# Last-factor products moved from VectorE to GpSimd, and a first load that no fill precedes, in a gated linear attention + multiplicative FFN kernel

## The chip, the cores and the metric

The kernel runs on one core of one Trainium2 chip. The time is device microseconds of one execution, as the median over several runs; beside it there is one profiled execution, whose trace gives every instruction's start and duration. Engines: PE is TensorE (PEld its weight loads), DVE is VectorE, ACT is ScalarE, POOL is GpSimd, SP is SyncE, which issues all of this kernel's DMAs.

## The reference

Two blocks in float32. The first is a gated linear recurrence over 768 positions for 4 x 8 heads of size 48; its result, laid out as 3072 rows of 384, goes through a feed-forward block that multiplies two up-projections.

```python
f = 1.0 / (1.0 + np.exp(-f_logit))
for t in range(S):
    state = f[:, :, t, :, None] * state + np.einsum('bhd,bhe->bhde', k[:, :, t], v[:, :, t])
    y[:, :, t] = np.einsum('bhd,bhde->bhe', q[:, :, t], state)
x = y.transpose(0, 2, 1, 3).reshape(B * S, H * D)
a = x @ w1
b = x @ w2
return ((a * b) @ w3) @ w_out
```

w1, w2, w3 and w_out come as float64 and are turned to float32 on the chip.

## The kernel before

The recurrence is cut into 24 chunks `u` of 128 positions, six to a batch (`NCH`). In a chunk, two heads share a tile: one on partitions 0 to 47, the other on 64 to 111, four such pairs side by side in 512 columns. Rows 48 to 63 between them belong to no head and are filled once: the loads' tiles `fs` with 30 (a gate of 1), `ks` and `qs` with 0.

**A chunk's steps**, each a task with a short name:

- `lf`, `lk`, `lq`, `lv`: loads of f_logit, k, q, v on SP's queue (`load`, L357 to L361, one DMA for each half of the partitions, issued at L360).
- `g`: the sigmoid on ACT into `gate` (L385). Two gate tiles alternate.
- `p`, `i`, `r`: a forward scan of products on VectorE (L393), a reciprocal of its last column (L403), a backward scan (L415). `l` copies the last column of the forward scan, the chunk's last factors, into `lasts` on ACT (L398).
- `q`, `k`: q and k scaled by the scans, on VectorE (L409; L424 in the first four chunks, L430 and L431 later).
- `a`, `t`: products of k and q, and transposes of k, on TensorE (L444, L456, L468). `m` copies the products to SBUF on ACT (L540, L543), `c` masks them causally on GpSimd (L549), `e` copies the transposed k (L568).
- `v`, `s`: values and the state's share on TensorE (L490, L502, L509), and the state's update into PSUM (L523).
- `d`: the new state `S` on VectorE, for all but the last chunk of a batch (`state`, L635 to L644). It first forms `G`, 112x4 numbers, the chunk's last factors times the first column of the next chunk's gates (L638). In the first chunk of a batch it multiplies the update by G (L641). In the others it adds the old S to the update (L643) and multiplies the sum by G (L644). `b` copies S into block form `sb` on ACT (L653), which the next chunk's state share reads.
- `y`, `z`, `x`: the result leaves PSUM (L663), is rearranged (L692 on TensorE for the first four chunks, through DRAM by DMAs later), and lands in `xt` (L697 or L687).

**The FFN** works on blocks of four chunks. Weights arrive as 64-bit words (L1093) and are decoded piece by piece: two steps on ACT (L1112, L1115) and four on VectorE (L1118, L1119, L1123, L1129). w3 and w_out are folded into one matrix `wc` (L1176, L1183). L714 issues nearly all FFN products; the first block uses plain products, later blocks a seven-product scheme whose sums are on VectorE (L784, L841, L852, L856, L950, L1208, L1222).

**The order** of all instructions is written by a planner (`Plan`, L75 to L150). Every task has an engine, an estimated cost, tasks that it depends on and a priority, its due time. `order` repeatedly takes the task that could start earliest, and of those that tie the one with the lowest priority number. The tasks are then emitted in that order, and each engine runs its own in order. In the task list, `d` costs 0.55 or 0.9 on VectorE, `c` 1.2 or 1.9 on GpSimd; `past(u, n, ...)` names tasks of the chunk n before, for buffers that are used again. Where TensorE has a planned gap in the first 35 planned us (`FULL`), the emission puts filler products there (L1278 to L1282, instruction at L277), one for each 0.43 planned us; nine stand at the very start. A matrix product in float32 is two instructions in the trace.

**Set-up** (`setup`, L284 to L310) is emitted ahead of all tasks: fills on GpSimd (L287 to L295), the identity matrix, constants on VectorE (L296 to L302), and on GpSimd a permutation matrix, filled (L304) and written in ten copies (L310).

**Who queues behind whom.** SP issues the loads in the planned order, the first f load ahead of everything. GpSimd's queue has only the set-up and then the masks `c`. `g` of chunk u waits for `d` of chunk u - 3, which read the same gate tile.

Of the kernel before, what the change touches and what calls it, by code (L numbers as in the profile page):

```python
# [50 lines left out]
R = 64 + D  # L51
# [138 lines left out]
def rows(par):  # L190
    return slice(64 * par, 64 * par + D)
# [15 lines left out]
def ranged(ctx, tc, q, k, f_logit, v, w1, w2, w3, w_out, out, ident, w12, wc, left):  # L207
# [76 lines left out]
    def setup():  # L284
        nc.scalar.activation(warm, nc.const_aps.tensor(0.0, (R, 1), F32), AF.Sigmoid)
        for i in range(2):
            nc.gpsimd.memset(fs[i][32:64], 30.0)  # L287
            nc.gpsimd.memset(ks[i][32:64], 0.0)
            nc.gpsimd.memset(qs[i][32:64], 0.0)
            if i == 0:  # L290
                make_identity(nc, ident)
        nc.gpsimd.memset(early[32:64, 2:4], 30.0)
        nc.gpsimd.memset(early[32:64, 0:2], 0.0)
        nc.gpsimd.memset(qs[2][32:64], 0.0)
        nc.gpsimd.memset(qs[3][32:64], 0.0)  # L295
        nc.vector.memset(floor, FLOOR)  # L296
        nc.vector.memset(heads(floor)[:, :, 0], 1.0)
        nc.vector.memset(back, 0.0)
        for t in gate:
            nc.vector.memset(t[:, NQ : NQ + 1], 0.0)  # L300
        for t in sb:
            nc.vector.memset(t, 0.0)  # L302

        nc.gpsimd.memset(perm, 0.0)  # L304
        for i, (kc, hp) in enumerate(met):
            for par in range(2):
                for r, t, at_, n in runs(2 * hp + par):
                    if t == kc:
                        a = 64 * par + at_
                        nc.gpsimd.tensor_copy(perm[:, i, r : r + n], ident[0:R, a : a + n])  # L310
# [19 lines left out]
    def past(u, n, *names):  # L330
        return [tk[u - n][nm] for nm in names if u >= n and nm in tk[u - n]]
# [20 lines left out]
    def front(u):  # L352
# [3 lines left out]

        def load(dst, src):  # L357
            def emit():
                for par in range(2):
                    nc.sync.dma_start(dst[rows(par)], src[u, par])  # L360
            return emit  # L361
# [22 lines left out]
        def gates():  # L384
            nc.scalar.activation(gate[u % 2][:, 0:NQ], fu, AF.Sigmoid)  # L385

        t["g"] = plan.add("ACT", 0.65, gates, [t["lf"]] + past(u, 2, "r") + past(u, 3, "d"), n0)
        if u % NCH and "d" in tk[u - 1]:
            tk[u - 1]["d"]["deps"].append(t["g"])

        def forward():
            s["P"] = one.tile([R, NQ], F32, name="fwd")
# [195 lines left out]
    def rest(u):  # L588
# [43 lines left out]
                paired(u + 1)  # L632

        if not closes:
            def state():  # L635
                s["S"] = work.tile([R, HP, D], F32, name="S")
                s["G"] = work.tile([R, HP], F32, name="G")
                nc.vector.tensor_tensor(s["G"], lasts[:, u], heads(gate[(u + 1) % 2][:, 0:NQ])[:, :, 0], ALU.mult)  # L638
                gain = s["G"].unsqueeze(2).to_broadcast([R, HP, D])
                if opens:  # L640
                    nc.vector.tensor_tensor(s["S"], s["pd"], gain, ALU.mult)  # L641
                else:
                    nc.vector.tensor_tensor(s["S"], s["pd"], st[u - 1]["S"], ALU.add)  # L643
                    nc.vector.tensor_tensor(s["S"], s["S"], gain, ALU.mult)  # L644

            t["d"] = plan.add(
                "DVE", 0.55 if opens else 0.9, state, [t["s"], t["l"]] + [tk[u + 1][nm] for nm in "g" if nm in tk[u + 1]] + past(u, 2, "b"), n0,
                frees=[] if u < NPE else [t["s"]],
            )

            def blocks():
                for par in range(2):
                    nc.scalar.copy(sb[u % 2][rows(par), :, 64 * par : 64 * par + D], s["S"][rows(par)])  # L653

            t["b"] = plan.add("ACT", 0.75, blocks, [t["d"]] + past(u, 1, "v"), n0)
# [967 lines left out]
```

## Time and profile before

| what | value |
|---|---|
| median of 4 runs | 489.72 us (489.52 to 489.87) |
| profiled execution | 489.65 us, span 487.8 us |
| VectorE: L638, the product G | x20, 131/155/1071 ns (min/median/max) |
| VectorE: L644 and L643, state | x16 at 357/358/359 ns; L643 mean 353 (x13) and 346 (x3) |
| VectorE: scans L393, L415 | x24 each, mean 1243 and 1234 ns |
| GpSimd: set-up copies L310 | x10, 191/218/1139 ns |
| GpSimd: masks L549 | 64x256 x80, mean 583 ns; 128x1024 x4, mean 1114 ns |

The span is what the profiler recorded of the program, from the first instruction to the last; the execution's time is 1.8 us longer. Of an engine's row in the groups, the duration is what the profiler recorded for one instruction, waits inside it for anything shared included; idle time in front of an instruction is shown with what released it.

### The profile page before, as it was taken

Reading aid. Unit: us, or ns where it says so; the run is one execution under the profiler, and the core shown is the slowest. Engines: PE = TensorE matmul, PEld = TensorE weight load, DVE = VectorE, ACT = ScalarE, POOL = GpSimd, SP = SyncE. Lnnn points to the kernel's source line nnn. Section 1 sums busy time; section 2 is a strip of 40 time slices with the busy share of each in tenths; the row PEclk is TensorE's granted clock in tenths of the full one; section 3 lists DMA queues with packets and bytes.
Section 4 is the critical chain, followed back from the end, with each engine's and each line's share of the span. In section 5 each row is a group of like instructions: output and inputs, shape, how many; then the busy total and the mean of one; then the engine's idle time right before and its main releaser. Section 6 shows DMA issues by size and latency. Waiting matters only on the chain.

```text
span 487.8 us, 9560 instructions
## 1 busy us (share of the span) xinstructions
PE 478.0 (98%) x3696; PEld 408.9 (84%) x3696; DVE 360.1 (74%) x721; ACT 166.0 (34%) x380; POOL 61.7 (13%) x115
## 2 busy tenths in 40 slices
PE   8899999999999999999999999999999999999995
PEld 7788744666799888899988888998899888889995
DVE  7999999999997689689877867456663667664541
ACT  4688456573234442544433441001100110110000
POOL 9110000305202111221311201000000000000000
PEclk9999999999999999999999999999999999999998
DMA  6889467563326553346542103000021000000011
GB/s 179 276 317 270 129 245 256 212 184 82 81 79 168 164 134 110 82 130 170 160 124 56 34 19 97 32 34 0 8 60 50 16 1 0 1 1 0 34 66 40
DMA packets 44920, 50.00 MB, mean 102 GB/s; under 512 B 15426, under 2 KB 34370, under 8 KB 43842
## 3 DMA queue, kind: packets, MB, share of 16 engines
q1 hardware_dynamic: 44866, 49.30, 33.8%
q8 instruction: 31, 0.51, 0.4%
q14 instruction: 23, 0.19, 0.1%
HBM read 40.63 MB, written 8.65 MB: 101 GB/s over the span
## 4 chain that ended last, share of the span: by engine, by line
PE 86%; DVE 6%; issue 1%; DVEq 0%
PE f L714 69%; PE f L1176 4%; PE py L490 4%; PE pa L456 2%; PE py L509 2%; PE py L468 2%; DVE place L1208 1%; PE f L523 1%; DVE place L1123 1%; DVE place L1129 1%; DVE bwd L415 1%; PE f L692 1%; DVE fwd L393 1%; DVE place L1222 0%; DVE place L950 0%
## 5 line engine op out<-in xcount | busy, mean ns | idle before, releaser
L714 PE MATMUL f<-xt,w 128*128 128x256 f32 (+1 forms) x600 | 159.0, 396 | 0.0
L714 PEld LDWEIGHTS f<-xt,w 128*128 128x128 f32 x600 | 113.5, 190 | 24.7 <-issue 10.8
L714 PE MATMUL f<-place 128*128 128x192 f32 (+1 forms) x504 | 112.4, 350 | 0.3 <-DVE place L950 0.3
L714 PEld LDWEIGHTS f<-place 128*128 128x128 f32 x504 | 87.9, 190 | 6.4 <-DVE place L950 0.6
L549 POOL TENSOR_SCALAR_AFFINE_SELECT A<-A 64x256 f32<-64x256 f32 (+1 forms) x84 | 49.4, 608 | 231.8 <-PE py L468 105.6
L1176 PE MATMUL f<-place 128*128 128x384 f32 x128 | 42.6, 489 | 0.5 <-DVE place L1129 0.5
L817 ACT COPY a<-f 128x256 f32<-128x256 f32 x36 | 13.4, 372 | 81.5 <-PE f L714 69.6
L1176 PEld LDWEIGHTS f<-place 128*128 128x128 f32 x128 | 23.9, 190 | 17.3 <-DVE place L1129 1.1
L714 PE MATMUL f<-xt,place 128*128 128x256 f32 x144 | 37.1, 380 | 0.0
L714 PE MATMUL f<-wc,ab 128*128 128x192 f32 x192 | 35.1, 326 | 0.0
L714 PEld LDWEIGHTS f<-wc,ab 128*128 128x128 f32 x192 | 32.0, 190 | 0.4
L393 DVE TENSOR_TENSOR_SCAN fwd<-gate,floor 112x512 f32<-112x512 f32 x24 | 29.8, 1243 | 2.4 <-ACT gate L385 1.9
L543 ACT COPY A<-pa 64x256 f32<-64x256 f32 (+1 forms) x60 | 24.3, 439 | 20.2 <-PE pa L456 19.6
L415 DVE TENSOR_TENSOR_SCAN bwd<-gate,back 112x512 f32<-112x512 f32 x24 | 29.6, 1234 | 0.7
L714 PEld LDWEIGHTS f<-xt,place 128*128 128x128 f32 x144 | 26.6, 189 | 3.5 <-DVE place L784 0.2
L841 DVE TENSOR_TENSOR place<-f,a 128x256 f32<-128x256 f32 x36 | 15.1, 421 | 18.8 <-PE f L714 18.5
L653 ACT COPY sb<-S 48x192 f32<-48x192 f32 x40 | 14.0, 350 | 27.5 <-DVE S L644 18.2
L490 PEld LDWEIGHTS py<-A,vt 128*64 128x64 f32 (+1 forms) x320 | 17.5, 129 | 6.7 <-issue 6.2
L1112 ACT ACTIVATE place<-place 128x512 f32<-128x512 f32 (+2 forms) x24 | 21.3, 888 | 3.9 <-DVE w L1129 2.0
L490 PE MATMUL py<-A,vt 128*64 128x128 f32 (+1 forms) x320 | 22.6, 281 | 0.0
L1115 ACT ACTIVATE place<-place 128x512 f32<-128x512 uint32 (+2 forms) x24 | 21.4, 896 | 1.4 <-DMA place<-in_w_out_dram 1.4
L714 PE MATMUL f<-place,w 128*128 128x256 f32 x72 | 21.4, 379 | 0.0
(119 smaller groups left out, 634.6 us busy)
## 6 DMA issues: line engine op xcount, KB each, us to landing
place<-in_w_dram SPq DMA_DIRECT2D x8, 1024.0 KB, 4.8
place<-in_w_dram SPq DMA_DIRECT2D x12, 512.0 KB, 9.5
out_dram<-o SPq DMA_DIRECT2D x24, 192.0 KB, 1.9
q<-in_q_dram SPq DMA_DIRECT2D x46, 96.0 KB, 2.3
f<-in_f_logit_dram SPq DMA_DIRECT2D x44, 96.0 KB, 2.3
k<-in_k_dram SPq DMA_DIRECT2D x44, 96.0 KB, 2.3
yt<-ys SPq DMA_DIRECT2D x40, 96.0 KB, 2.1
xt<-yt SPq DMA_DIRECT2D x20, 192.0 KB, 2.6
```

Of the source, the lines that this page charges most:

```text
L393: nc.vector.tensor_tensor_scan(s["P"], gate[u % 2][:, 0:NQ], floor, 0.0, ALU.mult, ALU.max)
L415: nc.vector.tensor_tensor_scan(s["R"][:, ::-1], gate[u % 2][:, NQ:0:-1], back[:, ::-1], 0.0, ALU.mult, ALU.max)
L490: nc.tensor.matmul(y_block(u, b)[64 * half : 64 * half + w], lhsT=s["v"][:, h * D : h * D + w], rhs=s["A"][:, par, hp], start=zone not in ...
L543: nc.scalar.copy(parts_of(s["A"].rearrange("p r h c -> p (r h c)"))[p0:p1, :, f], parts_of(s["pa"].rearrange("p r n -> p (r n)"))[p0:p1, : ...
L549: nc.gpsimd.affine_select(out=a, in_=a, pattern=pattern, compare_op=ALU.is_ge, fill=0.0, base=0, channel_multiplier=-1,)
L653: nc.scalar.copy(sb[u % 2][rows(par), :, 64 * par : 64 * par + D], s["S"][rows(par)])
L714: nc.tensor.matmul(out_, lhsT=lhs[i], rhs=rhs[i], start=start and i == 0, stop=i == len(lhs) - 1, skip_group_check=True,)
L817: nc.scalar.copy(q["a"], q["X"])
L841: nc.vector.tensor_tensor(ups["u3", k], q["Y"], q["a"], ALU.add)
L1112: nc.scalar.activation(m, hi.bitcast(F32), AF.Abs)
L1115: nc.scalar.activation(lo.bitcast(F32), lo, AF.Copy, bias=2.0, scale=2.0**-51)
L1176: nc.tensor.matmul(w3s["p", jc], lhsT=w3s[jc][:, kc * P : kc * P + P], rhs=wos[:, kc], start=(kc == 0), stop=(kc == KF - 1),)
```

## The change

The product G is taken out of `state` and becomes a GpSimd task of its own, `G`, with planned cost 0.3. It depends on `l`, on the next chunk's `g` if that is already in the list, and on `d` of two chunks before (its buffer). `d` depends on `s` and `G`; its planned cost falls to 0.36 or 0.72. Where `g` waited for `d` of three chunks before, or was added later to the previous `d`, it is now `G`.

In set-up, the fill of fs[0] is dropped: the first chunk's f load writes rows 0 to 63 in one DMA, the last 16 of them copies of the second half's first rows, and rows 64 to 111 in another. The fill of fs[1] now follows the identity. The fills of ks[1] and qs[1] move from GpSimd to VectorE.

```diff
         for i in range(2):
-            nc.gpsimd.memset(fs[i][32:64], 30.0)
-            nc.gpsimd.memset(ks[i][32:64], 0.0)
-            nc.gpsimd.memset(qs[i][32:64], 0.0)
             if i == 0:
+                nc.gpsimd.memset(ks[i][32:64], 0.0)
+                nc.gpsimd.memset(qs[i][32:64], 0.0)
                 make_identity(nc, ident)
+            else:
+                nc.gpsimd.memset(fs[i][32:64], 30.0)
...
         for t in gate:
             nc.vector.memset(t[:, NQ : NQ + 1], 0.0)
+        nc.vector.memset(ks[1][32:64], 0.0)
+        nc.vector.memset(qs[1][32:64], 0.0)
         for t in sb:
             nc.vector.memset(t, 0.0)
...
         def load(dst, src):
             def emit():
+                if dst is fs[0] and u == 0:
+
+                    nc.sync.dma_start(dst[0:64], src[u].rearrange("two d n -> (two d) n")[0:64])
+                    nc.sync.dma_start(dst[rows(1)], src[u, 1])
+                    return
                 for par in range(2):
                     nc.sync.dma_start(dst[rows(par)], src[u, par])
             return emit
...
-        t["g"] = plan.add("ACT", 0.65, gates, [t["lf"]] + past(u, 2, "r") + past(u, 3, "d"), n0)
-        if u % NCH and "d" in tk[u - 1]:
-            tk[u - 1]["d"]["deps"].append(t["g"])
+        t["g"] = plan.add("ACT", 0.65, gates, [t["lf"]] + past(u, 2, "r") + past(u, 3, "G"), n0)
+        if u % NCH and "G" in tk[u - 1]:
+            tk[u - 1]["G"]["deps"].append(t["g"])
...
         if not closes:
+            def gains():
+                s["G"] = work.tile([R, HP], F32, name="G")
+                nc.gpsimd.tensor_tensor(s["G"], lasts[:, u], heads(gate[(u + 1) % 2][:, 0:NQ])[:, :, 0], ALU.mult)
+
+            t["G"] = plan.add(
+                "POOL", 0.3, gains, [t["l"]] + [tk[u + 1][nm] for nm in "g" if nm in tk[u + 1]] + past(u, 2, "d"), n0,
+            )
+
             def state():
                 s["S"] = work.tile([R, HP, D], F32, name="S")
-                s["G"] = work.tile([R, HP], F32, name="G")
-                nc.vector.tensor_tensor(s["G"], lasts[:, u], heads(gate[(u + 1) % 2][:, 0:NQ])[:, :, 0], ALU.mult)
                 gain = s["G"].unsqueeze(2).to_broadcast([R, HP, D])
...
             t["d"] = plan.add(
-                "DVE", 0.55 if opens else 0.9, state, [t["s"], t["l"]] + [tk[u + 1][nm] for nm in "g" if nm in tk[u + 1]] + past(u, 2, "b"), n0,
+                "DVE", 0.36 if opens else 0.72, state, [t["s"], t["G"]] + past(u, 2, "b"), n0,
                 frees=[] if u < NPE else [t["s"]],
             )
```

## The prediction

> **What bounds the kernel now.** I read first the page's busy shares and its groups, then the tensor engine's waits, then a table of stages, then the first 36 us in order of time.
>
> ```profile
> PE 478.0 (98%) x3696; PEld 408.9 (84%) x3696; DVE 360.1 (74%) x721; ACT 166.0 (34%) x380; POOL 61.7 (13%) x115
> ```
>
> TensorE is busy all the time, so an edit on VectorE or GpSimd pays only where TensorE stops or does nothing useful. The table of stages says where (columns: stretch, its length, then busy time and count for PE, PEld, DVE, ACT, POOL, then clock and DMA):
>
> ```profile
> 8.30:35.50 27.20, 25.34 (x296) 21.86 (x295) 25.46 (x41) 19.75 (x41) 8.20 (x14) 1.00 0.88 292
> 35.50:77.00 41.50, 41.50 (x147) 27.51 (x147) 38.39 (x69) 25.75 (x43) 0.00 (x0) 1.00 0.70 218
> 77.00:135.00 58.00, 57.14 (x407) 36.92 (x405) 55.86 (x73) 29.29 (x54) 15.21 (x20) 1.00 0.50 155
> 135.00:482.40 347.40, 347.39 (x2834) 317.26 (x2834) 234.72 (x529) 88.28 (x239) 30.93 (x64) 1.00 0.23 64
> ```
>
> From 135.0 to 482.4 TensorE never stops (347.39 of 347.40). From 35.5 to 135 it stops 0.86 us in all. In 8.3 to 35.5 it stops 1.86 us, and its busy time there includes the filler multiplications of L277, 2.43 us at 10.68 and 1.04 us at 28.53: 1.86 + 2.43 + 1.04 = 5.3 us is all that this opening holds. The granted clock is 1.00 in all four rows. So the question is when the first up-projection (L714) can start, now 35.45.
>
> The opening in order of time, VectorE, GpSimd, ScalarE and SP together (start, duration, engine, line, operation):
>
> ```profile
> 0.81 0.52 POOL L287 MEMSET f<- 32x512 f32 x1 [0.29 <-POOLq L1610]
> 1.35 0.87 SPq L360 DMA_DIRECT2D f<-in_f_logit_dram  x2
> 4.08 0.63 ACT L385 ACTIVATE gate<-f 112x512 f32<-112x512 f32 x1 [1.77 <-DMA f<-in_f_logit_dram]
> 4.75 1.22 DVE L393 TENSOR_TENSOR_SCAN fwd<-gate,floor 112x512 f32<-112x512 f32 x1 [1.63 <-ACT gate L385]
> ...
> 7.97 4.07 POOL L310 COPY ab<-ident 112x48 f32<-112x48 f32 x10
> ...
> 12.13 1.09 POOL L549 TENSOR_SCALAR_AFFINE_SELECT A<-A 128x1024 f32<-128x1024 f32 x1
> 12.18 1.59 DVE L424 TENSOR_TENSOR K<-k,bwd 112x512 f32<-112x512 f32 x1
> ...
> 17.72 1.18 POOL L549 TENSOR_SCALAR_AFFINE_SELECT A<-A 128x1024 f32<-128x1024 f32 x1 [4.50 <-ACT A L540]
> 17.87 1.05 DVE L638 TENSOR_TENSOR G<-lasts,gate 112x4 f32<-112x4 f32 x1
> 18.84 0.34 DVE L643 TENSOR_TENSOR S<-py,S 112x192 f32<-112x192 f32 x1
> ...
> 24.19 1.09 POOL L549 TENSOR_SCALAR_AFFINE_SELECT A<-A 128x1024 f32<-128x1024 f32 x1 [5.29 <-ACT A L540]
> 24.23 1.07 DVE L638 TENSOR_TENSOR G<-lasts,gate 112x4 f32<-112x4 f32 x1
> ```
>
> The reader is to see two things. The first load is issued at 1.35, as the fill ends (0.81 + 0.52 = 1.33), and every gate, scan and scaling hangs on it. And a VectorE operation with two SBUF inputs that begins beside a GpSimd mask (L549) ends only after it: G takes 1.05 and 1.07 us where it takes 0.13 alone (11.64), K 1.59 where it takes 0.69. L643, which reads PSUM and SBUF, ran 0.34 at the tail of a mask. TensorE's view has what that costs:
>
> ```profile
> 19.24 0.60 PE L468 MATMUL py<-ident,K 112*128 112x112 f32 x4 [0.52 <-DVE S L643]
> ...
> 30.10 1.09 PE L490 MATMUL f<-A,place 128*64 128x128 f32 x16 [0.53 <-POOL A L549]
> ```
>
> **The change, part by part.** Times are of the profiled execution (489.65 us, span 487.84; the runs' median 489.72 is 0.07 above it).
>
> *First load.* Without the fill, SP is free at about 0.81, when ACT and POOL run their first instruction: the load moves 0.54 earlier at most, 0 if SP starts later; I take 0.5. SP issues its loads one behind another (0.42 us each, no pause up to 4.5), so k, q, v and the weights move too; their fills stay ahead of them (ks[0] now ends at 1.33, needed at 1.8). The first of the two DMAs grows from 48 to 64 rows, 32 KB on 192 KB, at the 2.3 us of an f load under 0.1 us. VectorE gets two fills in its place, like L298 0.49 each: its setup ends at 3.11 + 0.97 = 4.08, and the first scan now wants it at 4.75 - 0.5 = 4.25. The wait for the gate hides them with 0.17 to spare; without that cover they cost up to 0.97. TensorE hides 0.1 to 0.4 of the gain at first: its fillers of L277 run to 8.3, and the first transposes start at 8.34 either way.
>
> *G on GpSimd, its own price.* The trace has no two-input operation on GpSimd. From below: the copy L310 unblocked, 0.19; from above the same copy behind a scan, 1.14 (its maximum). I take 0.22, as 112x4 is smaller than those copies. G needs only lasts and the next gates, both there one to seven us before S, so in steady state its cost is 0 on the path; hidden by the update's matmuls, which S needs anyway.
>
> *G(0)* is the exception: it queues behind the ten setup copies, which now end at 12.05. Three fills less (3 x 0.46 = 1.4) bring them to 10.7, but copies wait for scans, so I take 11.4. Then G(0) ends at 11.6, and S(0), which VectorE could take at 11.72 - 0.5 = 11.2, starts at 11.65 instead of 11.90. K(1) comes at 12.0, finds mask(0) running (11.7 to 12.8) and ends near 13.3, not 13.77: turn(1) on TensorE gains **0.5**. Worst case: copies still end at 12.05, gain 0. Best: K(1) starts before the mask and ends at 12.2, gain 0.8, TensorE's own wait there.
>
> *G(1).* Its 1.05 us block goes: S(1)'s first half reads PSUM and runs at once. Turn(2) waits for that half (0.52), now for TensorE's z(0) instead: another **0.5**, sum 1.0. The second half (L644, two SBUF inputs) is late next: it waits out the mask in G's place, which delays only sb(1) on ACT, by then 1 us ahead.
>
> *G(2).* S(2) ended at 25.96, sb(2) went at 26.05 on ACT, and xt (0.48), a decode (0.69) and A(3) stood in order behind it, A(3) at 27.89. With VectorE 1 us earlier and no G, S(2) waits for mask(2) only and ends near 24.6; A(3) is then held by pairs(3) (26.2 - 1.0) and ACT's 0.48 + 0.73 behind it: start near 26.0, mask(3) ends at 28.2 instead of 30.05. TensorE's turn(3) and two fillers take until 28.1 to 28.5. So values(3) gains 1.6 at most; I take **0.5** on top of 1.0, because the decode may still stand ahead of A(3) (0.69).
>
> *Is the gain caught later?* The up-projection's second weights are the next late thing: the sixth decoded piece ends at 39.82 (L1129) and four products of 1.29 us after 35.45 need it at 40.6: 0.8 spare. Decoding is back to back on VectorE from 29.5 (2.12 a piece); it moves by VectorE's own gain, at least 1 us. 1.5 passes.
>
> *From 36 on.* VectorE loses 20 G's, 4.8 us, nearly all where TensorE never waits: 0. GpSimd gains 20 operations, 4.4 us, on an engine 13% busy; each can hold a two-input VectorE operation 0.22. In 77 to 135 that is three or four G's, under 0.9 us, on an engine that loses 0.16 for each: I take 0. The two stops (0.53 at 82.2, 0.34 at 134.7) stay: 0 to -0.87.
>
> *The planner.* VectorE's entry for S falls by 0.18 or 0.19, so a hand-made order is computed anew. The gap before turn(1), five fillers of 0.49, may lose one; I take 0.
>
> Sum: -(0.5 + 0.5 + 0.5) = -1.5. Span 486.3, run 488.15, against the median 488.2. Faster than 0.2% (0.98 us, about what a measurement of this kernel can tell from no change) begins at 488.74.
>
> The Trainium skill, SBUF — State Buffer, section "SBUF: two separate sides", says that VectorE with two SBUF inputs and a GpSimd operation that reads SBUF take one port pair in turns, the later one waiting out the whole instruction. The rows above agree (1.05 for 0.13), and the rule speaks against this change also: a G on GpSimd is one more such holder. GPSIMD Engine Reference, "4.1 Engine selection", puts two-input elementwise work on VectorE, GpSimd being about 2x slower; by it G would take an estimated 0.3 (2 x 0.155), and the sum would stay -1.5, since only G(0) is near the path.
>
> **Rivals.**
> *Nothing arrives* (0.25). G(0) stays behind the copies until 12.27, S(0) runs at 12.3 against 11.90, K(1) still meets the mask, and each later block moves from G to L644; the load's 0.5 is all that is left, or less. For it: ten copies in 4.07 us though one takes 0.22. Against: TensorE waited for L643, not L644. 489.0 to 489.8.
> *The new order costs in the decode stage* (0.15). Between 107.4 and 135 VectorE works 95% of the time and TensorE already waits 0.34 for L950: no slack. If the planner sets one chunk's two scans (1.24 + 1.24) ahead of the sums L1222 and L950, TensorE waits 2.5 longer: -1.5 + 2.5 = +1.0, 490.7. It decides once more than 1.5 us moves ahead. Against: scans stand in that order already.
> *More than the sum* (0.11). A filler goes (0.49) and both later stops close (0.87): 489.72 - 1.5 - 1.4 = 486.9.
>
> **How the numbers follow.** Forecast 0.49, own range 487.6 to 489.0 (a third of the sum either way). Of it 0.45 is faster by over 0.2%; with 0.11 from the larger gain and 0.03 from the top of "nothing" 0.59 faster; 0.26 same; 0.15 slower. The range for 8 in 10 reaches from the larger gain to the reorder: 486.9 to 490.7.
>
> **What would show it.** First f load near 0.85 and first scan near 4.25; turn(1) near 13.4; L638 on POOL at about 0.2 each; no VectorE operation over 1 us beside a mask in front of L643; values(3) near 28.6 and L714 from 34.0; busy shares past 36 as they are. Wrong, if G(0) ends after 12, if L714 starts after 35, or if TensorE's waits for VectorE between 77 and 135 grow past 1 us.

## The result, and the profile after

| | before | after |
|---|---|---|
| median of the runs | 489.72 us (60 runs) | 488.93 us (40 runs) |
| profiled execution | 489.65 us, span 487.8 | 488.89 us, span 486.6 |
| TensorE's last instruction ends | 482.40 | 481.02 |
| first up-projection product on TensorE | 35.55 | 34.80 |
| time of the execution less TensorE's end | 7.25 | 7.87 |

The ratio is 0.9985, with a 95% interval of 0.9981 to 0.9989: faster by 0.79 us, about half of the 1.5 us that were forecast, and inside the 0.2% that the prediction called no change. The table says in short where the rest is. TensorE ends 1.38 us sooner, nearly the forecast; 0.75 of it comes from the opening. Then 0.62 us go again *behind* TensorE's end, where the prediction had not looked. 1.38 - 0.62 = 0.76, the difference of the two profiled executions.

In the new file G is L645, the state's two halves are L657 and L658, the masks L557, the scaling of k L432, of q L417, the products of k and q L452, the values L498, the up-projection L728. First the busy shares:

```profile
PE 476.1 (98%) x3690; PEld 407.2 (84%) x3690; DVE 360.7 (74%) x703; ACT 166.0 (34%) x380; POOL 85.8 (18%) x132
```

VectorE lost 20 G's for two fills and its busy time did not fall (360.1 before); GpSimd's rose by 24 us for operations forecast at 4.4. The table of stages, cut at nearly the same places of the work (columns as before: length, then busy time and count for PE, PEld, DVE, ACT, POOL, then clock and DMA):

```profile
8.30:34.75 26.45, 23.53 (x288) 20.75 (x289) 25.16 (x39) 19.96 (x42) 9.53 (x15) 1.00 0.90 299
34.75:76.25 41.50, 41.50 (x147) 27.53 (x147) 38.56 (x68) 25.31 (x43) 1.48 (x2) 1.00 0.73 219
76.25:134.00 57.75, 57.57 (x410) 37.43 (x409) 55.94 (x73) 29.94 (x55) 17.15 (x22) 1.00 0.52 158
134.00:481.02 347.02, 347.02 (x2833) 316.50 (x2831) 234.46 (x514) 87.83 (x237) 50.24 (x77) 1.00 0.23 64
```

The opening is 0.75 shorter, although TensorE idles longer in it (26.45 - 23.53 = 2.92, before 1.86): the planner's new order has six filler instructions fewer, three fillers of 0.49. The decode stage idles 57.75 - 57.57 = 0.18 where it idled 0.86. The long last stage is as long as before: its row is 0.38 shorter because the cut at 134.00 lies 0.38 later in the work (TensorE's end is 1.38 sooner, and 135.00 - 1.38 = 133.62). Now the opening in order of time, lines of GpSimd, SP, ScalarE, VectorE and TensorE. As in the prediction, turn(n), pairs(n), values(n) and z(n) are TensorE's steps `t`, `a`, `v` and `z` of chunk n, mask(n) is GpSimd's `c`, and K(n), Q(n), S(n) and A(n) are tiles of chunk n.

```profile
0.82 0.59 SPq L364 DMA_DIRECT2D f<-in_f_logit_dram  x1
1.46 0.56 SPq L365 DMA_DIRECT2D f<-in_f_logit_dram  x1
...
4.18 0.63 ACT L393 ACTIVATE gate<-f 112x512 f32<-112x512 f32 x1 [1.87 <-DMA f<-in_f_logit_dram]
4.84 1.22 DVE L401 TENSOR_TENSOR_SCAN fwd<-gate,floor 112x512 f32<-112x512 f32 x1 [0.45 <-ACT gate L393]
...
6.58 5.25 POOL L313 COPY ab<-ident 112x48 f32<-112x48 f32 x10
...
11.80 0.19 POOL L645 TENSOR_TENSOR G<-lasts,gate 112x4 f32<-112x4 f32 x1
11.94 1.08 POOL L557 TENSOR_SCALAR_AFFINE_SELECT A<-A 128x1024 f32<-128x1024 f32 x1
12.03 0.36 DVE L655 TENSOR_TENSOR S<-py,G 112x192 f32<-112x192 f32 x1 [0.22 <-POOL G L645]
12.30 1.27 DVE L432 TENSOR_TENSOR K<-k,bwd 112x512 f32<-112x512 f32 x1
...
13.72 0.57 PE L476 MATMUL py<-ident,K 112*128 112x112 f32 x4 [1.05 <-DVE K L432]
```

The load is issued 0.53 sooner and lands no sooner. The set-up copies start earlier (6.58 instead of 7.97), but the ten take 5.25 instead of 4.07: five of them stand beside a scan or a scaling and take 0.66 to 1.18 each, where three did (0.69, 1.14, 1.14); G(0) starts at 11.80, and turn(1) at 13.72 against 13.91. Then chunks 1 and 2:

```profile
17.53 1.12 POOL L557 TENSOR_SCALAR_AFFINE_SELECT A<-A 128x1024 f32<-128x1024 f32 x1 [0.56 <-ACT A L548]
17.62 0.35 DVE L657 TENSOR_TENSOR S<-py,S 112x192 f32<-112x192 f32 x1
18.07 0.79 DVE L658 TENSOR_TENSOR S<-S,G 112x192 f32<-112x192 f32 x1
18.37 0.55 PE L476 MATMUL py<-ident,K 112*128 112x112 f32 x4
18.79 0.68 DVE L417 TENSOR_TENSOR Q<-q,fwd 112x512 f32<-112x512 f32 x1
...
19.61 1.16 PE L452 MATMUL pa<-Q,K 48*128 48x128 f32 x16 [0.70 <-ACT sb L667]
...
22.00 1.15 POOL L557 TENSOR_SCALAR_AFFINE_SELECT A<-A 128x1024 f32<-128x1024 f32 x1 [3.35 <-ACT A L548]
22.30 1.40 DVE L432 TENSOR_TENSOR K<-ab,bwd 112x512 f32<-112x512 f32 x1
...
24.45 1.16 PE L452 MATMUL pa<-Q,K 48*128 48x128 f32 x16 [1.00 <-DVE Q L417]
...
25.47 0.36 DVE L658 TENSOR_TENSOR S<-S,G 112x192 f32<-112x192 f32 x1
...
26.66 1.01 ACT L548 COPY A<-pa 128x1024 f32<-128x1024 f32 x1
```

S(1)'s first half no longer stands behind a blocked G, and turn(2) comes at 18.37 against 19.24: 0.87 ahead. That lead is not kept in full. The mask of chunk 1 now holds S(1)'s second half (0.79 for 0.36), and behind it Q(2) and the copy sb(1) start 0.43 later; the new order has put pairs(2), which reads Q(2), next on TensorE, and TensorE waits 0.70 there. The mask of chunk 2, which blocked G(2) before, now blocks K(3), which had been free:

```profile
23.02 0.69 DVE L424 TENSOR_TENSOR K<-ab,bwd 112x512 f32<-112x512 f32 x1
```

That is the line of before; K(3) takes 1.40 now, TensorE waits a whole microsecond for Q(3) behind it, and values(3) starts at 29.35 against 30.10, 0.75 ahead. The up-projection has the same 0.75.

### The profile page after: what moved, and what is told of

It is laid out like the page before. It is cut to its first block, busy times and chain, and to the rows that moved or that the text cites. A ratio compares the mean times of both kernels' runs of the same rounds, so it can differ in the third digit from the quotient of the medians.

```text
span 486.6 us, 9566 instructions
## 1 busy us (share of the span) xinstructions
PE 476.1 (98%) x3690; PEld 407.2 (84%) x3690; DVE 360.7 (74%) x703; ACT 166.0 (34%) x380; POOL 85.8 (18%) x132
## 4 chain that ended last, share of the span: by engine, by line
PE 88%; DVE 7%; POOL 2%; issue 1%; DVEq 0%; POOLq 0%
PE f L728 70%; PE f L1190 5%; PE py L498 4%; PE pa L464 2%; PE py L517 2%; PE py L476 2%; DVE place L1222 1%; PE f L531 1%; POOL ab L313 1%; DVE bwd L423 1%; DVE fwd L401 1%; PE f L706 1%; DVE Q L417 1%; DVE place L1137 0%; DVE place L1236 0%
## 5 line engine op out<-in xcount | busy, mean ns | idle before, releaser
L728 PE MATMUL f<-xt,w 128*128 128x256 f32 (+1 forms) x600 | 159.0, 396 | 0.0
L728 PEld LDWEIGHTS f<-xt,w 128*128 128x128 f32 x600 | 113.5, 190 | 24.8 <-issue 10.3
L728 PE MATMUL f<-place 128*128 128x192 f32 (+1 forms) x504 | 112.6, 350 | 0.2 <-DVE place L964 0.2
L728 PEld LDWEIGHTS f<-place 128*128 128x128 f32 x504 | 87.6, 190 | 6.2 <-DVE place L964 0.5
L557 POOL TENSOR_SCALAR_AFFINE_SELECT A<-A 64x256 f32<-64x256 f32 (+1 forms) x84 | 59.5, 728 | 90.4 <-ACT A L551 49.9
L831 ACT COPY a<-f 128x256 f32<-128x256 f32 x36 | 13.4, 372 | 85.0 <-PE f L728 66.0
L728 PE MATMUL f<-xt,place 128*128 128x256 f32 x144 | 37.3, 382 | 0.0
L728 PE MATMUL f<-wc,ab 128*128 128x192 f32 x192 | 35.1, 326 | 0.0
L645 POOL TENSOR_TENSOR G<-lasts,gate 112x4 f32<-112x4 f32 x20 | 14.3, 715 | 102.7 <-ACT lasts L406 39.8
L728 PEld LDWEIGHTS f<-wc,ab 128*128 128x128 f32 x192 | 32.0, 190 | 0.4
L728 PEld LDWEIGHTS f<-xt,place 128*128 128x128 f32 x144 | 26.6, 189 | 4.0 <-DVE place L855 0.5
L498 PEld LDWEIGHTS py<-A,vt 128*64 128x64 f32 (+1 forms) x320 | 17.5, 129 | 6.6 <-issue 6.1
L498 PE MATMUL py<-A,vt 128*64 128x128 f32 (+1 forms) x320 | 22.6, 280 | 0.0
L1129 ACT ACTIVATE place<-place 128x512 f32<-128x512 uint32 (+2 forms) x24 | 21.2, 889 | 1.8 <-DMA place<-in_w_out_dram 1.8
```

The lines of the kernel that those rows point to most:

```text
L498: nc.tensor.matmul(y_block(u, b)[64 * half : 64 * half + w], lhsT=s["v"][:, h * D : h * D + w], rhs=s["A"][:, par, hp], start=zone not in ...
L557: nc.gpsimd.affine_select(out=a, in_=a, pattern=pattern, compare_op=ALU.is_ge, fill=0.0, base=0, channel_multiplier=-1,)
L645: nc.gpsimd.tensor_tensor(s["G"], lasts[:, u], heads(gate[(u + 1) % 2][:, 0:NQ])[:, :, 0], ALU.mult)
L728: nc.tensor.matmul(out_, lhsT=lhs[i], rhs=rhs[i], start=start and i == 0, stop=i == len(lhs) - 1, skip_group_check=True,)
L1129: nc.scalar.activation(lo.bitcast(F32), lo, AF.Copy, bias=2.0, scale=2.0**-51)
```

## The experiments

Time less TensorE's end means, below, the profiled execution's time minus the end of its last matmul. Up-projection means its first instruction on TensorE. Both come from one execution of each kernel, and the opening differs from one execution to the next: before, before_pad and one_swap have the same instructions up to there, and reach the up-projection at 35.55, 35.77 and 35.37. So a difference of 0.3 there is not clear of chance by itself. The ratios come from all the runs.

### Taking the change apart

**setup_only**: the set-up and the first load alone, with G on VectorE inside `state` and the old order.

```diff
-            nc.gpsimd.memset(fs[i][32:64], 30.0)
-            nc.gpsimd.memset(ks[i][32:64], 0.0)
-            nc.gpsimd.memset(qs[i][32:64], 0.0)
             if i == 0:
+                nc.gpsimd.memset(ks[i][32:64], 0.0)
+                nc.gpsimd.memset(qs[i][32:64], 0.0)
                 make_identity(nc, ident)
+            else:
+                nc.gpsimd.memset(fs[i][32:64], 30.0)
...
+                if dst is fs[0] and u == 0:
+                    nc.sync.dma_start(dst[0:64], src[u].rearrange("two d n -> (two d) n")[0:64])
+                    nc.sync.dma_start(dst[rows(1)], src[u, 1])
+                    return
```

> The set-up part alone, G still on VectorE, the old order of tasks kept instruction for instruction. If the prediction's step on the first load holds (0.54 us earlier, handed on): first sigmoid near 3.6, first scan near 4.25, time -0.4 to -0.6 us against before. If the rival holds that the first DMAs land at a fixed time however early they are issued (the changed kernel's first sigmoid came at 4.18 against 4.08): first scan 4.8 to 4.9, time between -0.2 and +0.2 us.

**g_only**: the other part alone, G as a GpSimd task with the planner's new order, and the set-up and first load as before.

> The product on GpSimd as a planned task, with the new order that follows from it; old set-up. If all of the gain is the product's: -0.7 to -0.9 us against before, up-projections from 34.7. If the set-up part carries it: -0.3 us or less. The prediction's own two steps for G(1) and G(2) would give -1.0. Three fillers fewer at the matrix unit in either case, as the order is that of the changed kernel.

**gpool_oldorder**: G on GpSimd, while every other instruction keeps the old order; G is emitted as soon as its two inputs are.

```diff
+    def product(u, nm):
...
+        s["has"] = s.get("has", "") + nm
+        if len(s["has"]) == 2:
+            s["G"] = work.tile([R, HP], F32, name="G")
+            nc.gpsimd.tensor_tensor(s["G"], lasts[:, u], heads(gate[(u + 1) % 2][:, 0:NQ])[:, :, 0], ALU.mult)
...
```

> The product on GpSimd, but every other engine's instructions in the old order; old set-up. If the end of G's waits beside the masks is what pays (the prediction's G(1) and G(2)): -0.5 to -1.0 us, turn(2) near 18.3 to 18.7, fillers as before. If the order pays and the move itself does not: -0.2 to +0.2 us, because L644 waits out the mask in G's place.

**gdve_neworder**: the planner's new order, with G still computed by VectorE inside `state`; the GpSimd task is planned but emits nothing.

```diff
+            def gains():
+                pass
+
+            t["G"] = plan.add(
+                "POOL", 0.3, gains, [t["l"]] + [tk[u + 1][nm] for nm in "g" if nm in tk[u + 1]] + past(u, 2, "d"), n0,
+            )
...
```

> The new order of tasks, but G stays on VectorE, directly in front of S; old set-up. If the order pays: -0.4 to -0.9 us. If the move pays: -0.2 to +0.5 us, G again at over 1 us beside a mask in the opening.

Measured, in one table (us; stops are TensorE's idle time from 77 to 106 and from 106 to 140):

| kernel | median | ratio, 95% interval | turn(2) | up-projection | stops | TensorE's end |
|---|---|---|---|---|---|---|
| before | 489.66 (33 runs) | | 19.24 | 35.55 | 0.53, 0.34 | 482.40 |
| setup_only | 489.50 | 0.9995, 0.9985 to 1.0004 | 18.88 | 35.19 | 0.54, 0.35 | 482.06 |
| gpool_oldorder | 489.30 | 0.9993, 0.9984 to 1.0002 | 18.86 | 35.24 | 0.53, 0.35 | 482.10 |
| gdve_neworder | 489.24 | 0.9993, 0.9984 to 1.0002 | 19.22 | 35.49 | 0, 0.20 | 481.72 |
| g_only | 489.14 | 0.9988, 0.9979 to 0.9997 | 18.59 | 35.02 | 0, 0.18 | 481.27 |
| after | 488.93 | 0.9985, 0.9981 to 0.9989 | 18.37 | 34.80 | 0, 0.18 | 481.02 |

Of the parts alone only g_only's interval leaves no change out, so the split rests on the traces. At the up-projection the set-up brings 0.36, the move of G 0.31 and the new order 0.06: 0.73 of the 0.75. That they add up so well is partly chance: the scatter is as large, the profiled execution of gpool_oldorder (489.88) is 0.58 above its median, and set-up and g_only, taken together, make 0.36 + 0.53 = 0.89. One step is clear of chance. From turn(1) to turn(2) it is 5.32 to 5.34 in all six traces of this study with the opening's G's on VectorE, and 4.65 or 4.66 in all eight with them on GpSimd, in either order: the move brings 0.68 at turn(2). The two waits behind it, on the other hand, come from the new order, which has pairs(2) ahead of values(1), so that the mask of chunk 2 starts earlier (22.70 in gdve_neworder, 24.19 in before): K(3) takes 1.40 in gdve_neworder also, with G on VectorE, and 0.69 in every trace of the old order.

Of what was expected, setup_only went the rival's way (its sigmoid at 4.09, time -0.16), g_only (-0.52) and gpool_oldorder (-0.36) fell between their two cases, and gdve_neworder (-0.42) just reached "the order pays".

The later stops are clear too. The new order alone closes the first and halves the second, 0.69 of idle time and 0.63 at TensorE's end (1.38 - 0.75). In the old order they stay, with G on GpSimd too (one_swap, below, is the one exception); in all eight traces of the new order the first is 0 and the second 0.18 to 0.22, with G on VectorE too. So the step "From 36 on", which kept both stops, failed, and not through G's 4.8 us less on VectorE: VectorE is as busy as before there.

The same four kernels also say why GpSimd became busier. Its groups, first in gpool_oldorder, then in the kernel after (busy time, mean ns):

```profile
L359 POOL TENSOR_TENSOR G<-lasts,gate 112x4 f32<-112x4 f32 x20 | 7.3, 368 | 77.9 <-ACT lasts L408 36.8 <-ACT gate L394 18.7 <-PE f L723 10.8
```

```profile
L557 POOL TENSOR_SCALAR_AFFINE_SELECT A<-A 64x256 f32<-64x256 f32 x80 | 54.9, 708 | 81.9 <-ACT A L551 49.9 <-issue 23.3 <-PE f L728 7.4
L645 POOL TENSOR_TENSOR G<-lasts,gate 112x4 f32<-112x4 f32 x20 | 14.3, 715 | 102.7 <-ACT lasts L406 39.8 <-ACT gate L393 17.0 <-DVE back L411 14.7
```

G takes 0.19 or 0.20 when nothing is beside it and 0.72 on the average in the new order, where 14 of the 20 stand beside a scan, a scaling or a decoding step on VectorE and take 0.49 to 1.86; in the old order the mean is 0.37. The masks of the later chunks grew too (583 ns before, 708 after), and gdve_neworder, with no G on GpSimd, has 694: that is the order, not G. None of this is near the path.

### Which instruction closed the stop

**one_swap**: the kernel before with one instruction moved: the backward scan of chunk 4 one place forward on VectorE, ahead of the last sum L756.

```diff
+    tasks = plan.order()
+    r4 = tasks.index(tk[4]["r"])
+    on = [i for i in range(r4) if tasks[i]["eng"] == "DVE"][-1]
+    tasks.insert(on, tasks.pop(r4))
+    for t in tasks:
```

> The kernel before with one pair of VectorE instructions exchanged: the backward scan of chunk 4 ahead of the last product L756 instead of behind it. If this exchange is what closes TensorE's stop of 0.53 us in the first fold: that stop gone, up-projections at 35.5 as before, TensorE's end 0.4 to 0.6 us earlier, time -0.3 to -0.6 us. If the stop closed for another reason: no difference beyond 0.2 us.

The reason came from VectorE's order around 76 us. In the kernel after (there the sum is L770):

```profile
75.78 1.22 DVE L423 TENSOR_TENSOR_SCAN bwd<-gate,back 112x512 f32<-112x512 f32 x1
76.93 0.66 DVE L770 TENSOR_TENSOR ab<-f,ab 128x512 f32<-128x512 f32 x1
77.51 0.68 DVE L1132 TENSOR_SCALAR place<-place 128x1024 f32<-128x1024 f32 x1
```

In the kernel before the sum stood first, waited 0.41 for TensorE, and the scan and the decode of the fold's weights queued behind it:

```profile
77.15 0.69 DVE L756 TENSOR_TENSOR ab<-f,ab 128x512 f32<-128x512 f32 x1 [0.41 <-PE f L714]
77.76 1.21 DVE L415 TENSOR_TENSOR_SCAN bwd<-gate,back 112x512 f32<-112x512 f32 x1
78.89 0.67 DVE L1118 TENSOR_SCALAR place<-place 128x1024 f32<-128x1024 f32 x1
```

In one_swap the scan fills that wait:

```profile
76.59 1.23 DVE L415 TENSOR_TENSOR_SCAN bwd<-gate,back 112x512 f32<-112x512 f32 x1
77.73 0.67 DVE L756 TENSOR_TENSOR ab<-f,ab 128x512 f32<-128x512 f32 x1
78.31 0.69 DVE L1118 TENSOR_SCALAR place<-place 128x1024 f32<-128x1024 f32 x1
```

The decode starts at 78.31 and not at 78.89; 0.18 of this comes from the opening, 0.40 from the wait that is filled. TensorE's waits from 75 to 140 us in one_swap (total, times, longest):

```profile
PE f L714 <- DVE place L950: 0.3, 1, 0.3
PE f L1176 <- DVE place L1129: 0.2, 1, 0.2
```

The wait for L1129 fell from 0.53 to 0.16, and TensorE ended at 481.85 (before 482.40, of which 0.18 come from the opening). Median 489.37 against 489.81, ratio 0.9993 (0.9985 to 1.0002). One instruction moved into a wait that was there anyway does most of what the whole new order did to the first stop.

### The first load

**shape_only**: the kernel before, its fill still in front, with the first f load as 64 and 48 rows.

```diff
+                if dst is fs[0] and u == 0:
+                    nc.sync.dma_start(dst[0:64], src[u].rearrange("two d n -> (two d) n")[0:64])
+                    nc.sync.dma_start(dst[rows(1)], src[u, 1])
+                    return
```

> The kernel before with the first f load split as 64 and 48 rows, as in the change, with the fill kept in front and therefore the issue still at 1.35. Theory (the 64-row load itself is slower to issue and to land): the two issues take 0.56 to 0.60 instead of 0.40, the halves land at 4.0 and 4.6 instead of 3.53 and 3.97, the first sigmoid starts at 4.5 to 4.7 instead of 4.08. Rival (loads issued so early are slow whatever their shape): the issues take 0.40, landing and sigmoid as in the kernel before, within 0.1.

```profile
1.36 0.59 SPq L360 DMA_DIRECT2D f<-in_f_logit_dram  x1
2.00 0.56 SPq L361 DMA_DIRECT2D f<-in_f_logit_dram  x1
...
4.55 0.63 ACT L389 ACTIVATE gate<-f 112x512 f32<-112x512 f32 x1 [2.23 <-DMA f<-in_f_logit_dram]
```

Issued at 1.36, the same two DMAs take 0.59 and 0.56 again (0.40 and 0.41 as 48 rows each), and the sigmoid starts at 4.55; in the six traces with 48 rows each, issued at 1.35 or 1.36, it starts at 4.08 to 4.21. So the shape costs 0.34 to 0.47, most of the 0.53 that the earlier issue gained; loads so early are not slow for being early. Median 489.99 against 489.65, ratio 1.0007 (0.9997 to 1.0016). The profiled execution is the fastest of its ten (489.53), and in it the later sigmoid did not reach the up-projection (35.45).

**swap_halves**: the kernel after, with the two DMAs exchanged. The second half of the rows, which no fill touches, goes first; then the fill has ended, and rows 0 to 47 can go alone, 48 rows each.

```diff
+                nc.gpsimd.memset(fs[i][32:64], 30.0)
                 nc.gpsimd.memset(ks[i][32:64], 0.0)
...
-                    nc.sync.dma_start(dst[0:64], src[u].rearrange("two d n -> (two d) n")[0:64])
                     nc.sync.dma_start(dst[rows(1)], src[u, 1])
+                    nc.sync.dma_start(dst[rows(0)], src[u, 0])
```

> The changed kernel with the fill of fs[0] put back in front, but the first f load's two DMAs exchanged: the half on partitions 64 to 111, which no fill touches, goes first with 48 rows, the other after the fill. If a DMA of 48 rows issued at 0.82 lands as fast as before (2.17 us) and the shape of 64 rows was what cost: it lands near 3.0, the second near 3.5, first sigmoid near 3.6, time -0.3 to -0.5 us against the changed kernel. If nothing lands before about 3.5 however early it is issued: first landing near 3.5, second near 4.0, first sigmoid 4.1 to 4.2, time within 0.2 us of the changed kernel.

```profile
0.82 0.40 SPq L365 DMA_DIRECT2D f<-in_f_logit_dram  x1
1.36 0.33 SPq L366 DMA_DIRECT2D f<-in_f_logit_dram  x1
...
3.87 0.63 ACT L394 ACTIVATE gate<-f 112x512 f32<-112x512 f32 x1 [1.55 <-DMA f<-in_f_logit_dram]
```

The sigmoid comes at 3.87, between the two expectations (near 3.6, or 4.1 to 4.2), 0.31 sooner than in the kernel after, and everything follows by 0.30 to the up-projection (34.50). Median 488.74 against 489.81, ratio 0.9978 (0.9969 to 0.9987); the interval overlaps that of the change (0.9981 to 0.9989).

**late_table**: the kernel after, with ScalarE's first sigmoid put behind two fills of VectorE, to see whether the table load at 0.82 holds the first DMAs up.

```diff
-        nc.scalar.activation(warm, nc.const_aps.tensor(0.0, (R, 1), F32), AF.Sigmoid)
...
+        nc.scalar.copy(warm, floor[:, 0:1])
+        nc.scalar.activation(warm, warm, AF.Sigmoid)
```

> The changed kernel with ScalarE's first sigmoid, and perhaps its table load, put behind VectorE's first fills (near 1.65 us). If the table load, which ended at 2.10 in both kernels, holds the first load back: first f load lands near 3.0 and the second near 3.5. If it has no part in it: first landing 3.5 to 3.6 as in the changed kernel. If the table load does not move, the run says nothing.

It tells nothing: a table load still stood at 0.82 to 2.10, and a second one followed at 2.32. One execution, 488.66 us, the halves landing at 3.50 and 4.00. Whether a table load slows a DMA beside it stays open; shape_only accounts for most of the late landing without it.

### What took the G(2) step back

**fill_for_mask**: the kernel after, with the masks of the first four chunks replaced by fills with 0 of the same tile. It leaves out the products inside those four chunks.

```diff
             if u < NPE:
-                select(s["A"].rearrange("p r h c -> p (r h) c"), [[0, H], [1, C]])
+                nc.gpsimd.memset(s["A"].rearrange("p r h c -> p (r h c)"), 0.0)
                 return
```

> The changed kernel with the causal masks of the first four chunks replaced by fills of the same tile with 0 on GpSimd (the products inside those chunks are left out of the result); same order, same dependences, nearly the same length (a fill of 1024 columns took 0.94, a mask 1.09), but nothing is read. If the mask's reads are what hold VectorE in the opening: K at 0.69 in all four chunks (now 1.27 and 1.40 in two), L658 at 0.36 (now 0.79), up-projections 1.0 to 1.6 us earlier than in the changed kernel, time -0.8 to -1.5 us against it. If GpSimd's presence alone holds it, or the opening is bound elsewhere: up-projections within 0.3 us.

The fill of chunk 0 on GpSimd, and VectorE's operations beside this and the next two fills, in this kernel:

```profile
11.86 0.96 POOL L562 MEMSET A<- 128x1024 f32 x1
...
12.12 0.68 DVE L432 TENSOR_TENSOR K<-k,bwd 112x512 f32<-112x512 f32 x1
...
17.31 0.36 DVE L658 TENSOR_TENSOR S<-S,G 112x192 f32<-112x192 f32 x1
...
21.10 0.69 DVE L432 TENSOR_TENSOR K<-ab,bwd 112x512 f32<-112x512 f32 x1
```

A fill nearly as long as the mask (0.96 against 1.08) holds no one: K(1) takes 0.68 beside it (1.27 beside the mask), S(1)'s second half 0.36 (0.79), K(3) 0.69 (1.40). TensorE's wait in front of pairs(2) falls from 0.70 to 0.27, by the 0.43 that mask(1) had cost, and the one in front of pairs(3) from 1.00 to 0.30. Turn(1) comes at 12.95, the up-projection at 33.47, 1.33 before the kernel after; 0.18 of this is the first sigmoid's earlier start (4.00), which the fills have no part in. Median 487.68 against 489.81 (ratio 0.9960, 0.9948 to 0.9972). So what the masks block was still worth 1.1 to 1.3 us of the opening; the change moved the blocks and did not remove them. The Trainium skill, SBUF — State Buffer, section "SBUF: two separate sides", says as much: a VectorE operation with two SBUF inputs contends only with a GpSimd operation that reads SBUF, and the fill reads nothing.

**hold_mask2**: swap_g_early (below), with the mask of chunk 2 behind Q(3): emitted after it, and held by a one-column copy on GpSimd that reads Q(3).

```diff
             if u == 2:
+                nc.gpsimd.tensor_copy(warm, st[3]["Q"][:, 0:1])
...
+    tasks = plan.order()
+    c2 = tasks.pop(tasks.index(tk[2]["c"]))
+    tasks.insert(tasks.index(tk[3]["q"]) + 1, c2)
```

> The kernel of swap_g_early, with the mask of chunk 2 emitted after the scaling Q(3) and held back by a one-column copy on GpSimd that reads Q(3). Theory (the scaling K(3) meeting the mask of chunk 2 is what took the G(2) step back): K(3) takes 0.7 instead of 1.4, TensorE's wait of 1.0 for Q(3) shrinks to 0.3 or less, values(3) and the first up-projection come 0.5 to 0.8 us earlier than in swap_g_early, time -0.4 to -0.8 us. Rival (the mask itself is then late): values(2) waits for the mask by 0.7 to 1.3 us, the up-projection comes no earlier or up to 0.5 later. Rival (the gain is absorbed before the up-projection by sums, decoding or the fillers): K(3) is 0.7 and the up-projection moves by less than 0.2.

```profile
22.04 0.69 DVE L433 TENSOR_TENSOR K<-ab,bwd 112x512 f32<-112x512 f32 x1
...
23.48 1.16 PE L453 MATMUL pa<-Q,K 48*128 48x128 f32 x16 [0.30 <-ACT ys L686]
23.66 1.09 POOL L558 TENSOR_SCALAR_AFFINE_SELECT A<-A 128x1024 f32<-128x1024 f32 x1
23.70 1.32 DVE L1142 TENSOR_SCALAR place<-place 128x512 uint32<-128x512 uint32 x1
...
24.95 0.34 DVE L666 TENSOR_TENSOR S<-py,S 112x192 f32<-112x192 f32 x1
...
26.59 1.01 ACT L549 COPY A<-pa 128x1024 f32<-128x1024 f32 x1
```

K(3) is free and TensorE's wait in front of pairs(3) falls from 1.00 to 0.30. But the mask now meets the next VectorE operation that it can block, a step of the weights' decoding (1.32 for 0.43; the same step took 1.19 to 1.30 beside this mask in shape_only, gpool_oldorder and before_pad), and S(2) behind it is at 24.95, later than in swap_g_early (24.66). A(3), which ScalarE copies after it has copied S(2), goes at 26.59 against 26.31. Values(3) and the up-projection come only 0.12 sooner (28.88, 34.33). The third expectation held: K(3) is free, and the gain is gone before the up-projection. Median 487.72 against 489.65 (ratio 0.9959, 0.9945 to 0.9972), not to be told from swap_g_early.

### Behind TensorE's end

The time less TensorE's end had been 7.23 to 7.25 in before, one_swap and gdve_neworder, 7.58 in setup_only (its last store landed 0.3 later), and 7.67 to 7.89 in all kernels with all 20 G's on GpSimd. GpSimd's closing instructions stand still once in some of these. Their starts, in us after TensorE's end, worked out from the traces (drain, clearing of the semaphores, drain, two last semaphore instructions):

```
before            4.90  5.01  5.18  5.26  5.33
after             5.03  5.14  5.31  5.39  5.47
swap_halves       4.98  5.09  5.26  5.34  5.74
gpool_oldorder    5.19  5.30  5.47  5.87  5.96
g_only            4.96  5.07  5.56  5.78  5.87
```

A pause of 0.32 (0.40, 0.40 and 0.49 between two starts that are 0.08, 0.08 and 0.17 apart in before) moves forward by an instruction as GpSimd's program grows: recorded instructions there, those of semaphores and issue included, are 172 in before, 186 in after, 187 in swap_halves, 188 in gpool_oldorder, 189 in g_only. In the kernel after no pause is recorded, but the execution outlasts its span by more (2.33, before 1.74, table below); in gpool_oldorder and g_only, whose pause lies well inside the span, it does not (medians 1.79 and 1.84). Two kernels tested whether the length of GpSimd's program does it.

**before_pad**: the kernel before, and 15 fills of one column on GpSimd in chunk 12's mask task, read by nobody.

```diff
+            if u == 12:
+                for _ in range(15):
+                    nc.gpsimd.memset(warm, 0.0)
```

> The kernel before with 15 fills of one column by GpSimd, in chunk 12's mask task, far from any wait of TensorE; nobody reads them. Theory (program length on GpSimd): TensorE's end stays at 482.4 within 0.1 and the time less TensorE's end rises from 7.25 to 7.65 to 7.9, time +0.4 to +0.5 us. Rival (G's own waits and semaphores, not the number of instructions, cost the time behind TensorE's end): time less TensorE's end stays 7.25 within 0.1, time unchanged within 0.15 us.

**swap_g_early**: swap_halves with G on GpSimd in the first six chunks alone, and on VectorE, inside the state's task, later.

```diff
+            def gains():
+                if u < NCH:
+                    product(nc.gpsimd)
...
+                if u >= NCH:
+                    product(nc.vector)
```

> The kernel of swap_halves (the change with the first f load's halves exchanged), with G on GpSimd only in the first batch's chunks (u below 6) and back on VectorE, inside the state's task, in the later ones; the plan is the same. GpSimd's program loses 15 instructions. Theory (the longer program on GpSimd is what takes 0.4 to 0.5 us back between TensorE's end and the run's end): TensorE ends at 480.8 within 0.2 as in swap_halves, and the time less TensorE's end falls from 7.9 to 7.2 to 7.4, so the time falls by 0.4 to 0.5 us against swap_halves, to about 0.9970 of the kernel before. Rival (what lies behind TensorE's end has nothing to do with G): time less TensorE's end stays at 7.7 to 7.9, ratio 0.9978 as in swap_halves. Rival (G on GpSimd helps in the later chunks also): TensorE ends later than 481.0.

Measured: the profiled execution's time less TensorE's end, and over all runs how far the execution outlasts its span:

| kernel | instructions recorded on GpSimd | time less TensorE's end | time less span, median (lowest to highest), runs |
|---|---|---|---|
| before, beside before_pad | 172 | 7.25 | 1.74 (1.67 to 1.83), 22 |
| before_pad | 185 | 7.59 | 2.01 (1.99 to 2.11), 11 |
| after | 186 | 7.87 | 2.33 (2.21 to 2.49), 42 |
| swap_halves | 187 | 7.85 | 1.94 (1.89 to 2.01), 11 |
| swap_g_early | 176 | 7.20 | 1.71 (1.67 to 1.83), 6 |
| hold_mask2 | 176 | 7.32 | 1.69 (1.67 to 1.82), 5 |

Fifteen idle fills bring extra time into the kernel before, 0.34 where 0.40 to 0.65 were expected; fifteen G's fewer take all of it out, as expected (TensorE's end 480.67 against 480.76, time less TensorE's end 7.20 against 7.85). So G's own waits are not needed for it: instructions on GpSimd that nobody waits for bring it as well. Why 185 recorded instructions cost 0.34 and 186 to 189 of them 0.42 to 0.64 was not found out. before_pad's median rose by more, 490.21 against 489.65 (ratio 1.0007, 0.9998 to 1.0016); in its profiled execution 0.22 more come from the opening, far ahead of the fills, where ScalarE waited 1.39 for weight words and TensorE 0.83 for ScalarE.

swap_g_early takes 487.95 against 489.65 us, ratio 0.9966 (0.9954 to 0.9978). Its interval lies below that of the change as made (0.9985, 0.9981 to 0.9989) and overlaps that of swap_halves: another 0.2%, from the load's halves and from 15 G's fewer on GpSimd together. hold_mask2 has the lowest ratio of the kernels that compute the whole result, 0.9959, inside the same interval.

## Why the prediction was half right

- **First load, 0.5.** No term of the sum, but part of the first one, turn(1). Mis-sized: the sigmoid gained nothing (4.18; 3.58 would have been the 0.5). The earlier issue was right (0.82), but the 64 rows were priced by their bytes, "under 0.1". The first DMA took 0.19 longer to issue, the second 0.15; shape_only shows the shape alone costing 0.34 to 0.47. The two fills on VectorE were hidden, as said. setup_only's 0.36 at the up-projection did not come through the gate (4.09 against 4.08), but through K(1), which took 1.22 for 1.59 as mask(0) ended earlier; its turn(1) was 0.37 ahead.
- **G's own price, 0.22.** The floor was right (0.19), the use was not: mean 0.72, which cost nothing. The factor of two in the Trainium skill, GPSIMD Engine Reference, section "4.1 Engine selection", had given an estimate of 0.3, no nearer to the mean: what stands beside G decides (0.19 to 1.86).
- **Turn(1) by G(0), 0.5.** The worst case named for it nearly came: copies to 11.83, G(0) ending at 11.99, K(1) at 12.30 in the mask. Turn(1) gained 0.19. "I take 11.4" for the copies was the step that failed: moved 1.4 earlier, they ran into one scan and one scaling more and took 1.18 longer.
- **G(1), 0.5.** Right, and larger: turn(2) gained 0.68 on top of turn(1)'s 0.19, so 0.87 of the sum of 1.0. L644's successor L658 waits out the mask (0.79), as said. That this "delays only sb(1)" was wrong: in the new order pairs(2) is next on TensorE, and it came 0.43 later for it.
- **G(2), 0.5.** It brought nothing: -0.12, within the scatter (turn(2) to values(3) is 10.50 to 11.16 in the old order's traces, 10.97 to 10.99 in the new order's with G on GpSimd and the masks as they were). The prediction had S(2) "waits for mask(2) only and ends near 24.6"; it ended at 25.83, since K(3) met the mask and the new order put two decoding steps ahead of it. A(3) started at 26.66 instead of 26.0. Together, the masks of chunks 1 and 2 held pairs(3) up by 0.43 and 0.71. And it was not K(3) as such: hold_mask2 freed K(3) and the same mask blocked a decoding step. In before_pad and shape_only, whose order is the old one, the mask happened to come later and G(2) missed it (0.15 each, 1.07 in before); S(2)'s first half ran at 24.23 and 24.57 instead of 25.22, yet values(3) came at 30.32 and 30.00 against 30.10, behind TensorE's own queue (turn(3) at 28.97 and 28.65, before 28.14). An earlier S(2) alone did not bring values(3) forward there.
- **"Is the gain caught later".** Right: the 0.75 of values(3) is there at the up-projection and at the second stage's end, unchanged.
- **From 36 on, 0.** Wrong to the good side, 0.63 at TensorE's end: the first stop closed and the second was halved. The clause "0 to -0.87" held the case; the prediction put it beside a lost filler as a rival with a chance of 0.11. The cause is the planner's new order (gdve_neworder), for the first stop one scan in a wait (one_swap). The second stop's fall, 0.34 to 0.18, goes with the new order as well; which instruction does it was not tried.
- **The planner, 0.** Three fillers went, not one, and pairs(2) went ahead of values(1). TensorE's idle time took the fillers' place; the up-projection gained 0.06 from the order alone, which is no change within the scatter.
- **Not in the prediction:** the 0.62 behind TensorE's end. The sum was made for the span and then carried over to the time with a fixed 1.8 between them; that distance grew to 2.3. The span alone fell by 1.24.

So the three terms of the sum were 0.19, 0.68 and -0.12 (0.75 for 1.5), 0.63 came from the two stops, and 0.62 went behind TensorE's end. The last two were not in the sum, and it is luck that they cancel; what is left, the opening's missing 0.75, put the time near the upper end of the forecast's own range, 0.07 below the range of the rival "nothing arrives". Of the signs named in advance the issue of the first load (0.82) came. The first scan (4.84 for 4.25), turn(1) (13.72 for 13.4), G at about 0.2 each (mean 0.72), values(3) (29.35 for 28.6) and no VectorE operation over 1 us beside a mask (K(3)) did not. None of the three limits that would have called it wrong was passed, G(0)'s end (11.99 of 12) by 0.01. Of the rivals, "nothing arrives" had the right places (copies, K(1) in the mask, the block moved to L644), and its answer fell short because turn(2) hangs on L643, as the objection to it said.

## What to carry over

When two engines block each other for whole instructions, taking one instruction away moves the block to the next one that qualifies: price the move by what then stands beside the mask, or take away what blocks (here a GpSimd operation that reads SBUF), which was worth another 1.1 to 1.3 us; moving one kind of victim had brought 0.68 at turn(2) and, alone, 0.31 at the up-projection. A changed cost in a planner is a change of its own: build it alone, since here the new order by itself brought 0.63 in two stops that the move did not touch, and in the opening took back some of what the move had gained. And compare the time less the last useful instruction's end as well as the span; the instructions added on GpSimd far from the end were paid for behind it.

## What was not expected of the hardware

- A first DMA of 64 rows of 512 floats took 0.59 to issue and its successor of 48 rows 0.56, where two of 48 rows took 0.40 and 0.41 or 0.33; with the issue at 1.35 or 1.36 in both, the sigmoid started 0.34 to 0.47 later.
- With 185 instructions or more on GpSimd instead of 172 to 176, an execution took 0.34 to 0.65 longer behind TensorE's end. In three kernels (187, 188 and 189) the trace shows GpSimd's closing instructions paused for 0.32, one instruction earlier for each instruction more. That instructions without any use bring the extra time was shown (before_pad, 0.34); its cause, the fetching of instructions for example, was not.
- A decoding step with one SBUF input (L1142 in hold_mask2, 128x512 uint32) took 1.32 beside a mask and 0.43 otherwise, and 1.19 to 1.30 beside one in three other kernels: not only two-input operations are held. The Trainium skill, SBUF — State Buffer, section "SBUF: two separate sides", counts operations in a two-port performance mode in as well; whether this step runs in one, no run here shows.
